# A fused attention, expert routing and feed-forward kernel: routing tables, sigmoids, transposes and the last search rearranged

## Chip, cores and metric

One core of a Trainium2 chip runs the whole program. The metric is the device time of one execution in microseconds (us), as the median of several runs.

## The reference

Three stages follow one another. Four batches of 768 positions with 8 heads of 40 make 32 (batch, head) pairs and 3072 tokens of width 320.

```python
# 1 attention, per (batch, head), step by step over t
m_new = max(f_gate + m, i_gate);  f = exp(f_gate + m - m_new);  i = exp(i_gate - m_new)
C = f*C + i*outer(v, k);  n = f*n + i*k
y = sigmoid(o_gate) * (C @ q) / max(|n . q|, 1)
# 2 routing with a capacity of 3072/8 = 384 tokens for each expert, then the expert
logits = x @ w_gate          # 8 experts
for idx in argsort(-logits.flatten()):      # best pair first
    if token not assigned and expert not full: assign
x[mask_e] = relu(x[mask_e] @ w1[e]) @ w2[e]
# 3 a gated feed-forward for all tokens
out = (sigmoid(x @ w_gate2) * (x @ w_val)) @ w_out
```

## The kernel before

**Attention** works in 6 chunks of 128 positions. A chunk has three head groups of 12, 12 and 8 (batch, head) pairs, so there are 18 steps `j`, with `c, s = divmod(j, 3)`. Within a chunk the recurrence is written as a masked matrix. For four heads at a time, `decay` (L209) makes the exponents in a PSUM tile `pg` (two buffers) with matmuls, and ScalarE turns them into weights with four `Exp` instructions (L220) in an SBUF tile `ee` (seven buffers). `score` (L223) multiplies them by q times k, `outp` (L269) applies them to v, `inter` and `state` carry the state from chunk to chunk, and `comb` (L280) multiplies by the output gate `ON[c]`, a sigmoid of a whole 128x1280 tile (`sig`, L136), on GpSimd. `gates` (L139) makes the running maxima and sums on VectorE, once for chunk 0 and once for chunks 1 to 5 together. The mask matrix `tris` (L442) is read by every `decay`.

`xout` (L298) normalizes the output y; `half` (L325) stores it to DRAM and calls `flip` (L315), which transposes blocks of 128 columns into the PSUM tile `tr` (one buffer) and copies them to the SBUF tile `xt` (one buffer). `lmm` (L331) makes the routing logits from `xt`, and `Routing.start` (L536) reduces the logits of one chunk and compares them with the first table.

`step` (L365) walks a fixed list of calls (`ORDER`, L363), in which decays run two steps ahead of the step that they belong to. In this part of the program the order of instructions on each engine is not the order of the code: a planner simulates the program and picks, of the instructions that are ready, the one traced first. Only dependencies and buffers bind it.

`Attention.run` (L343) traces the constants of the routing (`Routing.consts`, L436: 23 small VectorE instructions and 7 on GpSimd, among them the six tables `tab` of L452) ahead of everything else, then `setup` (L50: loads of the gates, of the first step's keys, queries and values, a GpSimd fill of the two key tiles `kb` at L62, the load of the first output gate, `gates(0, 1)`), `setup2` (L100: a GpSimd fill and six small loads of the router's weight `wgt`), step -1 (only decays and scores of the first steps), the sigmoid of chunk 0, steps 0 and 1, the lambdas, and steps 2 to 18. From step 2 on, `prep_moe2` (L731) is called at each `s` of the list: it splits the weights of stage 3 into pairs of numbers. The output gates of the later chunks are loaded at `LO` and put through the sigmoid at `SG`, at the end of chunks 0, 2 and 4.

**Routing and experts** run in a hand-written order (`manual_schedule`, L1120). The eight experts are taken in the order in which they fill up. `Routing.phase(i)` (L543) finds which expert is next and the logit at which it is full: six rounds, each with a comparison of all best logits with a table of thresholds on VectorE (L533), 24 small matmuls that count (L587) and one that spreads the result (L597). It then makes the list of the expert's 384 tokens (L652 to L686), and `gather` (L910) fetches them by indirect DMA. The phase for expert i+1 is a generator that `drive` (L1093) advances by one `yield` at each `yield` of `Ffn.run(i)` (L964), so that its work lies between the matmuls of expert i.

`Ffn.run(i)` does the two expert matrices (L977 to L1002) and then stage 3 in 12 blocks `f` of 128 columns: gate and value matmuls (L955 to L962), sigmoid (L1050), product (L1062), a split into two parts (L1063, L1057), and, two blocks later, nine matmuls (L1071 to L1073) that add block k = f - 2 to three token tiles `oc[tb]`. At the end each token tile is copied to SBUF (L1081, L1083) and written out by an indirect DMA from GpSimd (L1085).

Of the kernel before, what the change touches and what calls it, by code (L numbers as in the profile page):

```python
# [40 lines left out]
class Attention:  # L41

    def __init__(self, ctx, tc, g, a, xd):
        self.tc, self.nc, self.g, self.a, self.xd = tc, tc.nc, g, a, xd
        self.one = ctx.enter_context(tc.tile_pool(name="a_one", bufs=1))
        self.wk = ctx.enter_context(tc.tile_pool(name="a_work", bufs=2))
        self.ps = ctx.enter_context(tc.tile_pool(name="a_psum", bufs=1, space=bass.MemoryType.PSUM))
        self.ON, self.QT, self.W, self.X, self.XT, self.T1, self.Y, self.PO = {}, {}, {}, {}, {}, {}, {}, {}

    def setup(self):  # L50
# [10 lines left out]
        for t in self.KB:  # L61
            nc.gpsimd.memset(t, 0.0)  # L62
        self.load(0, "kqv")
        self.load_o(0)
# [3 lines left out]
        self.load(1, "kqv")  # L68
        self.KW = one.tile([L, HS, D], FT, name="kw")
# [66 lines left out]
    def sig(self, c):  # L136
        self.nc.scalar.activation(self.ON[c], self.ON[c], AF.Sigmoid)

    def gates(self, c0, c1):  # L139
# [40 lines left out]
        nc.vector.tensor_copy(self.GB[64:96, sl], G[64:96, sl])  # L180
# [28 lines left out]
    def decay(self, j, k):  # L209
        nc = self.nc  # L210
        c, s = divmod(j, NS)
        h0 = s * HS + 4 * k
        pg = self.ps.tile([L, 4, L], FT, name="pg", bufs=2)
        nc.tensor.matmul(pg, self.g["R"].tris, self.negi[:, None, :].to_broadcast([L, 4, L]), start=True, stop=False)
        for h in range(4):
            nc.tensor.matmul(pg[:, h, :], self.sel[:, h0 + h:h0 + h + 1].to_broadcast([96, L]),  # L216
                             self.GB[:, c * L:(c + 1) * L], start=False, stop=(h == 3))
        ee = self.wk.tile([L, 4, L], FT, name="ee", bufs=7)
        for h in range(4):
            nc.scalar.activation(ee[:, h, :], pg[:, h, :], AF.Exp, bias=self.GT[:, c, h0 + h:h0 + h + 1])  # L220
        self.W[j, k] = ee
# [93 lines left out]
    def flip(self, c, z, i0, n):  # L315
        nc = self.nc
        xf = self.xf(c, z)
        if i0 == 0:
            self.XT[c, z] = self.wk.tile([L, 5, 128], FT, name="xt", bufs=1)
        p = self.ps.tile([L, 4, 128], FT, name="tr", bufs=1)  # L320
        for i in range(n):
            nc.tensor.transpose(p[:, i, :], xf[:, 128 * (i0 + i):128 * (i0 + i) + 128], self.g["ident"])
        nc.scalar.activation(self.XT[c, z][:, i0:i0 + n], p[:, :n], AF.Copy)
# [7 lines left out]
    def lmm(self, c, z, i0, n):  # L331
        if i0 == 0:
            self.PL = self.ps.tile([L, 7, 2, E], FT, name="pic", bufs=2)
        for i in range(i0, i0 + n):
            self.nc.tensor.matmul(self.PL, self.XT[c, z][:, i, :], self.wgt[:, i][:, None].to_broadcast([L, 7, 2, E]),
                                  start=(i == 0), stop=(i == 4))
# [28 lines left out]
    def step(self, j, side):  # L365
# [7 lines left out]
        if j == -1:  # L373
            for k in range(n1):
                self.decay(0, k)
        for t in self.ORDER:
            if t == "L" and cur and nx2:
                self.load(j + 2, "kqv")
            elif t == "LO" and cur and s < 2 and c % 2 == 0 and c + 1 + s < NC:
# [21 lines left out]
            elif t == "KW" and nxt:  # L401
                self.kw(j + 1)
            elif t in ("S0", "S1", "S2") and nxt and int(t[1]) < n1:
                self.score(j + 1, int(t[1]))
            elif t == "H2" and hv:
                self.half2(*hv, 2 if j == last else 0)
                if j == last - 1:
                    self.store(NC - 1, 1, 0)
                    self.flip(NC - 1, 1, 0, 2)
                if hv[1]:  # L410
                    self.g["R"].start(hv[0])
            elif t == "SG" and cur and s == NS - 1 and c % 2 == 0:
                for z in range(c + 1, min(c + 3, NC)):
                    self.sig(z)
            elif t == "s":
                side(1)


class Routing:
# [15 lines left out]

    def consts(self, tmp):  # L436
# [4 lines left out]
        self.tris = one.tile([128, 128], BF, name="tris")  # L441
        nc.vector.tensor_scalar(self.tris, jp, 0.0, None, op0=OP.is_gt)  # L442
# [100 lines left out]
    def phase(self, i, on_e, on_x):  # L543
        nc, wk = self.nc, self.wk
        v, t8, A, cmp = self.v, self.t8, self.A, self.cmp
        last = i == E - 1

        def be(t):
            return t[:, :, None].to_broadcast([128, NJ, E])

        if i:
            yield from self.best(slice(0, NJ), i)
# [51 lines left out]
        ts = tx.bitcast(FT)  # L604
# [9 lines left out]

        nc.vector.tensor_scalar(gg[:, 0], v, ts, None, op0=OP.is_ge)
        nc.vector.tensor_tensor(ag, A, be(gg[:, 0]), op=OP.mult)
        with nc.allow_low_precision(reason="counts up to 24 are exact in bfloat16"):
            nc.vector.tensor_reduce(sm[:, 0], ag.rearrange("p j e -> p e j"), axis=AX.X, op=OP.add)
        nc.vector.tensor_scalar(st, v, ts, None, op0=OP.is_gt)
        nc.vector.tensor_sub(td, gg[:, 0], st)  # L620
        yield
        yield
        yield
        p = self.ps(i)
        nc.tensor.matmul(p[:, 0:E], self.ones, sm[:, 0], start=True, stop=True)
        if i:
            nc.vector.tensor_tensor(st, st, self.act, op=OP.mult)
            nc.vector.tensor_tensor(td, td, self.act, op=OP.mult)
        nc.vector.tensor_tensor(ta, t8, st, op=OP.mult)
        nc.vector.tensor_add(self.asg, self.asg, ta)  # L630
# [3 lines left out]
        nc.vector.tensor_tensor(es, p[:, 0:E], self.rem, op=OP.is_ge)  # L634
        nc.vector.tensor_tensor(es, es, self.we[:, 0], op=OP.mult)
        nc.vector.tensor_reduce(mx, es, axis=AX.X, op=OP.max)
# [11 lines left out]
        nc.vector.tensor_scalar(esb, es, mx, None, op0=OP.is_equal)  # L648
# [57 lines left out]
class Ffn:  # L706
# [257 lines left out]
    def run(self, i):  # L964
# [73 lines left out]
        for f in range(12 + LAG):  # L1038
# [27 lines left out]
            if k >= 0:  # L1066
# [117 lines left out]
```

## Time and profile before

| | |
|---|---|
| median of 3 runs | 866.32 us (865.43 to 867.01) |
| the profiled execution, its own time | 863.38 us |
| its span, first to last instruction | 861.6 us |
| TensorE (PE) busy | 803.2 us, 93% |
| VectorE (DVE) busy | 541.1 us, 63% |
| ScalarE (ACT) busy | 340.6 us, 40% |
| GpSimd (POOL) busy | 234.1 us, 27% |
| mean granted TensorE clock | 0.973 of full speed |

The span starts at 0. Attention reaches to about 200 us, the first routing search to about 223 us, and the eight experts from there to the end. A row of a timeline gives start and duration, the line in the code, the operation, output tile and inputs, sizes, and in brackets the idle time of the engine ahead of it with what ended it. Starts of consecutive matmuls lie closer than their durations, because they are pipelined: the distance of the starts is what one costs. SPq is the queue that issues the loads.

### The profile page before, as it was taken

How to read it: one execution, taken by the hardware profiler on the slowest of the kernel's cores; microseconds unless marked ns; L12 is line 12 of the kernel's file. 1: busy time of each engine (PE TensorE's matmuls, PEld its weight loads, DVE VectorE, ACT ScalarE, POOL GpSimd, SP SyncE). 2: the span in 40 equal slices, each digit the busy share in tenths (PEclk: the TensorE clock that was granted, in tenths of full speed). 3: DMA queues.
4: the chain of work that ended last, by engine and by line, in shares of the span. 5: the costliest groups of instructions: out<-in, count | busy, mean ns of one | idle time of the engine just before them, and what ended most of it. 6: DMA issues, size and time to landing. Idle time of an engine off the chain costs nothing.

```text
span 861.6 us, 16078 instructions
## 1 busy us (share of the span) xinstructions
PE 803.2 (93%) x6200; PEld 763.4 (89%) x6200; DVE 541.1 (63%) x1438; ACT 340.6 (40%) x755; POOL 234.1 (27%) x255
## 2 busy tenths in 40 slices
PE   4979888994699999999999999999999999999996
PEld 3978788893589999999999999999999999999996
DVE  7988988956576576656666566556566665642321
ACT  4776696520342342252234225222513442252321
POOL 3244444510210260071036006301710450072001
PEclk8999989996799999999999999999999999999998
DMA  5687666400400410310050014004000500130000
GB/s 151 207 266 227 197 210 198 155 29 31 135 24 1 143 40 2 112 46 24 2 158 24 1 36 123 24 2 128 30 24 2 158 24 1 60 99 24 1 1 23
DMA packets 40951, 67.66 MB, mean 79 GB/s; under 512 B 5066, under 2 KB 29386, under 8 KB 40874
## 3 DMA queue, kind: packets, MB, share of 16 engines
q1 hardware_dynamic: 38426, 58.72, 22.4%
q0 software_dynamic: 2304, 7.87, 2.8%
q8 instruction: 48, 0.79, 0.4%
q14 instruction: 29, 0.24, 0.1%
q10 hardware_dynamic: 144, 0.05, 0.0%
HBM read 58.76 MB, written 7.86 MB: 77 GB/s over the span
## 4 chain that ended last, share of the span: by engine, by line
PE 71%; DVE 2%; DMA 2%; issue 1%; ACT 1%; SPq 1%; POOL 1%; POOLq 0%; ACTq 0%; DVEq 0%
PE mm L955 8%; PE mm L956 8%; PE mm L957 8%; PE mm L977 7%; PE mm L962 5%; PE ac L1071 5%; PE mm L961 5%; PE ac L1073 5%; PE ac L1072 5%; PE rp L587 3%; PE ac L994 3%; PE ac L996 3%; PE ac L995 3%; PE ac L1000 1%; PE ac L999 1%; DMA ws<-in_moe_w_dram 1%
## 5 line engine op out<-in xcount | busy, mean ns | idle before, releaser
L955 PE MATMUL mm<-yh,mh 128*128 128x384 f32 x384 | 134.3, 350 | 0.0
L956 PE MATMUL mm<-yh,ml 128*128 128x384 f32 x384 | 129.3, 337 | 0.0
L957 PE MATMUL mm<-yl,mh 128*128 128x384 f32 x384 | 129.2, 337 | 0.0
L915 POOL DMA_INDIRECT xg<-xd,ix x24 | 23.8, 992 | 376.8 <-DVE scr L682 372.0
L1057 DVE TENSOR_TENSOR gl<-gf,gh 128x384 fp32r<-128x384 f32 x96 | 77.2, 804 | 37.3 <-ACT gh L1063 37.0
L1050 ACT ACTIVATE sg<-mm 128x384 f32<-128x384 f32 x96 | 47.1, 490 | 133.0 <-PE mm L962 133.0
L1063 ACT ACTIVATE gh<-gf 128x384 fp32r<-128x384 f32 x96 | 50.2, 523 | 114.2 <-DVE gf L1062 114.2
L1071 PE MATMUL ac<-oh,gh 128*128 128x320 f32 x288 | 92.6, 322 | 0.0
L1073 PE MATMUL ac<-oh,gl 128*128 128x320 f32 x288 | 89.3, 310 | 0.7 <-DVE gl L1057 0.7
L1072 PE MATMUL ac<-ol,gh 128*128 128x320 f32 x288 | 89.2, 310 | 0.0
L1062 DVE TENSOR_TENSOR gf<-sg,mm 128x384 f32<-128x384 f32 x96 | 52.7, 549 | 52.2 <-ACT sg L1050 51.6
L985 ACT ACTIVATE gh<-mm 128x384 fp32r<-128x384 f32 x64 | 31.3, 491 | 117.8 <-PE ac L1000 51.1
L955 PEld LDWEIGHTS mm<-yh,mh 128*128 128x128 f32 x384 | 72.6, 189 | 0.2 <-DVE xl L896 0.2
L956 PEld LDWEIGHTS mm<-yh,ml 128*128 128x128 f32 x384 | 72.7, 189 | 0.0
L957 PEld LDWEIGHTS mm<-yl,mh 128*128 128x128 f32 x384 | 72.3, 188 | 0.0
L962 PE MATMUL mm<-pad,mr 128*128 128x384 f32 x192 | 64.8, 338 | 0.0
L961 PE MATMUL mm<-y,m 128*128 128x384 f32 x192 | 64.6, 336 | 0.0
L220 ACT ACTIVATE ee<-pg,GT 128x128 f32<-128x128 f32 x192 | 53.9, 370 | 11.8 <-PE pg L216 11.4
L229 PE MATMUL s<-qT,kb 120*128 120x128 f32 x384 | 56.0, 292 | 2.7 <-DVE ee L230 2.4
L1073 PEld LDWEIGHTS ac<-oh,gl 128*128 128x128 f32 x288 | 54.2, 188 | 0.9 <-DVE gl L1057 0.9
L1071 PEld LDWEIGHTS ac<-oh,gh 128*128 128x128 f32 x288 | 54.6, 190 | 0.0
L278 PE MATMUL po<-vn,ee 128*128 128x123 f32 (+2 forms) x384 | 52.3, 284 | 2.2 <-DVE ee L230 2.2
(281 smaller groups left out, 1919.5 us busy)
## 6 DMA issues: line engine op xcount, KB each, us to landing
ws<-in_moe_w_dram SPq DMA_DIRECT2D x15, 480.0 KB
ws<-in_moe_w_dram SPq DMA_DIRECT2D x14, 512.0 KB
ws<-in_moe_w_dram SPq DMA_DIRECT2D x18, 256.0 KB
on<-in_on_dram SPq DMA_DIRECT2D x6, 640.0 KB
xd<-y SPq DMA_DIRECT2D x24, 160.0 KB
st<-in_moe_w_out_dram SPq DMA_DIRECT2D x12, 320.0 KB
st<-in_moe_w_gate_dram SPq DMA_DIRECT2D x8, 384.0 KB
st<-in_moe_w_val_dram SPq DMA_DIRECT2D x8, 384.0 KB
```

Of the source, the lines that this page charges most:

```text
L220: nc.scalar.activation(ee[:, h, :], pg[:, h, :], AF.Exp, bias=self.GT[:, c, h0 + h:h0 + h + 1])
L229: nc.tensor.matmul(s[:, h, :], self.KB[j % 2][:, a, r, :], self.QT[j][:, a, :], start=True, stop=True)
L955: mm(p, wh[:, d, cs], h[:, d], start=(d == 0), stop=False)
L956: mm(p, wl[:, d, cs], h[:, d], start=False, stop=False)
L957: mm(p, wh[:, d, cs], l[:, d], start=False, stop=False)
L961: mm(p, w2[:, cs], x[2], start=False, stop=False)
L962: mm(p, wr[:, c2], self.pad[z], start=False, stop=True)
L977: mm(p, (self.al if t == 1 else self.ah)[:, d, cs], x[t // 2][:, d], start=(d == 0 and t == 0), stop=False)
L1057: nc.vector.tensor_tensor(gl, hs[f - 1][0], hs[f - 1][1].bitcast(FT), op=OP.subtract)
L1071: mm(o, gh[:, ts], self.oh[:, k], start=(k == 0), stop=False)
L1072: mm(o, gh[:, ts], self.ol[:, k], start=False, stop=False)
L1073: mm(o, gl[:, ts], self.oh[:, k], start=False, stop=(k == 11))
```

## The change

- **Routing tables.** `Routing.consts` is traced after step 1 instead of first, its temporary tiles move to the pool that opens after the gates' pool closes, and each of its VectorE instructions is held by an ordering edge (`issue_after`) behind the last VectorE instruction of `gates(0, 1)`. `tris` is made early, by a function of its own. `setup2` moves behind step 1, too.
- **Start.** The fills of `kb` go from GpSimd to ScalarE, as copies of the identity scaled by 0. The first loads come in the order q, v, k. Step -1 is written out: `kw(0)`, decays and scores of step 0, decays of step 1, then step 0. The output gate of chunk 0 is loaded in step 0.
- **Sigmoids.** They come in pairs, in step 0 and at the end of chunks 1 and 3. An edge holds a pair behind the last `Exp` traced, and the `Exp` of the next four `decay` calls are held behind the pair. Output gates are loaded in odd chunks.
- **Last chunk's transposes** use `pg` (two buffers) instead of `tr` in PSUM, and tiles of the `ee` pool instead of `xt` in SBUF, one for each call of `flip`.
- **Last expert.** The phase for expert 7 does not search: all tokens still active go to it. It yields as often as before (`sum(...) + 3` empty yields).
- **End.** In the last expert's stage 3 the blocks k = 10 and 11 are added token tile by token tile, in place of block by block.

```diff
@@ Attention.setup, sig, decay, flip
-            nc.gpsimd.memset(t, 0.0)
-        self.load(0, "kqv")
-        self.load_o(0)
+            nc.scalar.activation(t.rearrange("p a r t -> p (a r) t"), g["ident"][:GP, None, :].to_broadcast([GP, 12, L]),
+                                 AF.Copy, scale=0.0)
+        self.load(0, "qvk")
...
+        g["R"].strict(g["jp"])
...
+    def sig2(self, c0, c1):
+        tc = self.tc
+        with tc.issue_after(self.lastexp):
+            ins = self.sig(c0)
+        for c in range(c0 + 1, c1):
+            with tc.issue_after(ins):
+                ins = self.sig(c)
+        self.behind = [ins, 4]
...
+        ins, n = self.behind
+        with self.tc.issue_after(ins) if n else nullcontext():
+            for h in range(4):
+                e = nc.scalar.activation(ee[:, h, :], pg[:, h, :], AF.Exp, bias=self.GT[:, c, h0 + h:h0 + h + 1])
+        self.lastexp = e.ins
+        self.behind[1] = max(0, n - 1)
...
+        end = c == NC - 1
+        p = self.ps.tile([L, 4, 128], FT, name="pg" if end else "tr", bufs=2 if end else 1)
...
+        if end:
+            t = self.wk.tile([L, 4, L], FT, name="ee", bufs=7)
@@ Attention.run
-            rt.consts(self.gp)
             self.setup()
-            self.setup2()
+            self.kw(0)
+            for k in range(GK[0]):
+                self.decay(0, k)
+                self.score(0, k)
+            gend = self.gend
             g1 = self.gates(1, NC)
-            self.step(-1, lambda n: None)
-            self.sig(0)
+            for k in range(GK[1]):
+                self.decay(1, k)
             self.step(0, lambda n: [next(g1, 0) for _ in range(2 * n)])
...
             self.step(1, lambda n: None)
+            self.setup2()
             self.lambdas()
         with self.tc.tile_pool(name="a_conv", bufs=1) as cv:
+            with self.tc.issue_after(gend):
+                rt.consts(cv)
@@ Attention.step
-            elif t == "LO" and cur and s < 2 and c % 2 == 0 and c + 1 + s < NC:
+            elif t == "LO" and j == 0:
+                self.load_o(0)
+                self.load_o(1)
+                self.sig2(0, 2)
+            elif t == "LO" and cur and s < 2 and c % 2 and c + 1 + s < NC:
...
-            elif t == "SG" and cur and s == NS - 1 and c % 2 == 0:
-                for z in range(c + 1, min(c + 3, NC)):
-                    self.sig(z)
+            elif t == "SG" and cur and s == NS - 1 and c % 2:
+                if c + 1 < NC:
+                    self.sig2(c + 1, c + 3)
@@ Routing.phase
+        ts = None
+        if not last:
+            ts = yield from self.search(i)
...
+        if last:
+            nc.vector.memset(td, 0.0)
+            nc.vector.tensor_tensor(ta, t8, self.act, op=OP.mult)
+            nc.vector.tensor_add(self.asg, self.asg, ta)
+            nc.vector.tensor_copy(mx, t8[:, 0:1])
+            for _ in range(sum(3 if n > 31 else 2 for n, _, _ in self.tab) + len(self.tab) + 3):
+                yield
@@ Ffn.run
-            if k >= 0:
+            if i == E - 1 and f >= 12:
+                if f == 13:
+                    for tb in range(3):
+                        ts = slice(tb * 128, tb * 128 + 128)
+                        o = oc[tb][:, :HD]
+                        for k in (10, 11):
+                            gl, gh = hs[k]
+                            mm(o, gh[:, ts], self.oh[:, k], start=False, stop=False)
+                            mm(o, gh[:, ts], self.ol[:, k], start=False, stop=False)
+                            mm(o, gl[:, ts], self.oh[:, k], start=False, stop=(k == 11))
+            elif k >= 0:
```

## Rows read from the trace of the kernel before

**Rows 1.** Busy time by stage: stretch, length, PE, PEld, DVE, ACT, POOL, clock, DMA.

```profile
16.00:45.00 29.00, 26.32 (x216) 23.92 (x216) 25.32 (x47) 23.43 (x65) 7.00 (x10) 0.88 0.67 207
45.00:90.00 45.00, 38.82 (x332) 35.96 (x331) 41.25 (x85) 30.18 (x86) 19.76 (x21) 0.96 0.77 248
...
180.00:193.00 13.00, 12.81 (x116) 12.69 (x115) 8.78 (x20) 1.21 (x4) 2.24 (x2) 1.00 0.01 1
...
400.00:500.00 100.00, 100.00 (x792) 95.61 (x792) 61.59 (x175) 32.66 (x63) 20.94 (x19) 1.00 0.13 40
```

**Rows 2.** PE's timeline in expert 6, around one round of the search.

```profile
710.99 0.76 PE L587 MATMUL rp<-A,cmp 128*128 128x8 bf16 x24
...
711.87 0.34 PE L977 MATMUL mm<-xh,al 128*128 128x384 f32 x1
712.04 0.34 PE L977 MATMUL mm<-xl,ah 128*128 128x384 f32 x1
...
713.09 0.18 PE L597 MATMUL rp<-sat,ones 128*128 128x1 bf16 x1
...
713.38 0.34 PE L977 MATMUL mm<-xh,al 128*128 128x384 f32 x1
```

**Rows 3.** All waits of PE from 700 to 860 us: total, times, longest.

```profile
PE mm L924 <- DMA xg<-xd,ix: 0.5, 1, 0.5
```

**Rows 4.** PE's timeline, first and last of its last 18 matmuls.

```profile
850.61 0.31 PE L1071 MATMUL ac<-oh,gh 128*128 128x320 f32 x1
...
853.11 0.31 PE L1073 MATMUL ac<-oh,gl 128*128 128x320 f32 x1
```

**Rows 5.** Timelines of DVE and POOL at the end of the span.

```profile
850.87 0.56 DVE L1057 TENSOR_TENSOR gl<-gf,gh 128x384 fp32r<-128x384 f32 x1 [0.59 <-ACT gh L1063]
...
853.29 0.97 POOL L1085 DMA_INDIRECT out_dram<-xg,ix  x1 [67.96 <-ACT xg L1083]
...
855.83 0.97 POOL L1085 DMA_INDIRECT out_dram<-xg,ix  x1 [0.22 <-issue]
```

**Rows 6.** PE's timeline, end of attention: last transposes and router matmuls.

```profile
193.53 0.66 PE L322 MATMUL tr<-ident,y 128*128 128x128 f32 x4 [0.73 <-DVE y L306]
194.94 0.33 PE L322 MATMUL tr<-ident,y 128*128 128x128 f32 x1 [0.75 <-ACT xt L323]
...
197.12 0.70 PE L335 MATMUL pic<-wgt,xt 128*128 128x112 f32 x4 [0.53 <-ACT xt L323]
...
198.73 0.92 PE L335 MATMUL pic<-wgt,xt 128*128 128x112 f32 x6 [0.58 <-ACT xt L323]
```

**Rows 7.** DVE's timeline at the start.

```profile
1.45 3.43 DVE L442 TENSOR_SCALAR tris<-jp 128x128 bf16<-128x128 f32 x1
...
5.32 0.18 DVE L499 TENSOR_SCALAR k<-tab 128x63 int32<-128x63 int32 x1
...
6.49 0.48 DVE L144 TENSOR_TENSOR_SCAN m<-gt,m 96x128 f32<-96x128 f32 x1
...
10.69 0.90 DVE L180 CAST GB<-G 32x128 bf16<-32x128 f32 x1
16.13 1.55 DVE L144 TENSOR_TENSOR_SCAN m<-gt,m 96x640 f32<-96x640 f32 x1 [4.54 <-DMA gt<-in_f_gate_dram]
```

**Rows 8.** Timelines of ACT and POOL at the start.

```profile
10.42 1.28 ACT L137 ACT_TABLE_LOAD   x1
...
16.96 5.62 ACT L220 ACTIVATE ee<-pg,GT 128x128 f32<-128x128 f32 x20
...
2.12 2.68 POOL L62 MEMSET kb<- 120x1536 f32 x2
```

**Rows 9.** Groups of ACT instructions by line, 0 to 195 us: the sigmoids and their table loads.

```profile
L137 ACT ACT_TABLE_LOAD x6 | 7.7, 1283 | 4.1 <-DMA on<-in_on_dram 4.0
L137 ACT ACTIVATE on<-on 128x1280 f32<-128x1280 f32 x6 | 7.6, 1271 | 2.7 <-DMA on<-in_on_dram 2.7
```

**Rows 10.** PE's timeline: the longest wait for an exp behind a sigmoid.

```profile
59.92 0.38 PE L214 MATMUL pg<-negi,tris 128*128 128x512 bf16 x1 [2.68 <-ACT ee L220]
```

More of the change, by code (lines that the diff above doesn't have):

```diff
@@ L1 @@
-from contextlib import ExitStack
+from contextlib import ExitStack, nullcontext
 import concourse.bass as bass
@@ L434, in alloc, with strict @@
             self.nc.gpsimd.memset(t, 0.0)
+    def strict(self, jp):
+        self.tris = self.one.tile([128, 128], BF, name="tris")
+        self.nc.vector.tensor_scalar(self.tris, jp, 0.0, None, op0=OP.is_gt)
     def consts(self, tmp):
@@ L541, in start, with search @@
         self.compare(sl, tab, n)
[L543 to L552, printed above, removed]
+    def search(self, i):
+        nc, wk, A, cmp = self.nc, self.wk, self.A, self.cmp
         P = wk.tile([128, 1], I32, name="P")
@@ L603, in phase, with be @@
         nc.vector.tensor_tensor(tx, tx, dg, op=OP.bitwise_xor)
-        ts = tx.bitcast(FT)
+        return tx.bitcast(FT)
+    def phase(self, i, on_e, on_x):
+        nc, wk = self.nc, self.wk
+        v, t8, A, cmp = self.v, self.t8, self.A, self.cmp
+        last = i == E - 1
+        def be(t):
+            return t[:, :, None].to_broadcast([128, NJ, E])
+        if i:
+            yield from self.best(slice(0, NJ), i)
+        ts = None
+        if not last:
+            ts = yield from self.search(i)
         gg = wk.tile([128, 3, NJ], BF, name="gg")
@@ L633, in phase @@
         esb = wk.tile([128, E], BF, name="esb")
-        nc.vector.tensor_tensor(es, p[:, 0:E], self.rem, op=OP.is_ge)
-        nc.vector.tensor_tensor(es, es, self.we[:, 0], op=OP.mult)
-        nc.vector.tensor_reduce(mx, es, axis=AX.X, op=OP.max)
+        if last:
[5 more added lines that the diff above has]
+                yield
+        else:
+            nc.vector.tensor_scalar(gg[:, 0], v, ts, None, op0=OP.is_ge)
+            nc.vector.tensor_tensor(ag, A, be(gg[:, 0]), op=OP.mult)
+            with nc.allow_low_precision(reason="counts up to 24 are exact in bfloat16"):
+                nc.vector.tensor_reduce(sm[:, 0], ag.rearrange("p j e -> p e j"), axis=AX.X, op=OP.add)
+            nc.vector.tensor_scalar(st, v, ts, None, op0=OP.is_gt)
+            nc.vector.tensor_sub(td, gg[:, 0], st)
+            yield
+            yield
+            yield
+            p = self.ps(i)
+            nc.tensor.matmul(p[:, 0:E], self.ones, sm[:, 0], start=True, stop=True)
+            if i:
+                nc.vector.tensor_tensor(st, st, self.act, op=OP.mult)
+                nc.vector.tensor_tensor(td, td, self.act, op=OP.mult)
+            nc.vector.tensor_tensor(ta, t8, st, op=OP.mult)
+            nc.vector.tensor_add(self.asg, self.asg, ta)
+            nc.vector.tensor_tensor(es, p[:, 0:E], self.rem, op=OP.is_ge)
+            nc.vector.tensor_tensor(es, es, self.we[:, 0], op=OP.mult)
+            nc.vector.tensor_reduce(mx, es, axis=AX.X, op=OP.max)
         mm = self.mmp[:, 1:2 * NJ + 1]
@@ L647, in phase @@
         on_e()
-        nc.vector.tensor_scalar(esb, es, mx, None, op0=OP.is_equal)
+        if not last:
+            nc.vector.tensor_scalar(esb, es, mx, None, op0=OP.is_equal)
         yield
```

41 lines of the change are left out of this document (11 added, 30 removed).

## The prediction

> **What bounds the kernel now.** I read the busy time by stage first, then the waits and timelines of the places that the change touches.
>
> The stages have different limits [rows 1]. In the expert stage (400 to 500 us) PE is busy for all of 100.00 us at full clock; DVE has 61.59, ACT 32.66. What leaves PE's queue there comes off the time; what leaves another engine does not. The steady part of attention (45 to 90 us) has two engines near their limit, DVE with 41.25 and PE with 38.82 of 45 us, and no DMA limit. The start (16 to 45 us) is like it, at a mean clock of 0.88. In the last 13 us of attention PE is the bound again, 12.81 of 13.
>
> **The last search.** The change takes six rounds of the search out of expert 6's run, where PE is full; its only wait from 700 to 860 us is 0.5 us for a gather [rows 3]. In a round the 24 small matmuls start at 710.99 and the second wide matmul behind them at 711.87: 0.88 us, of which one wide slot (712.04 - 711.87 = 0.17) is the work of expert 6, so 0.71 us are the search's [rows 2]. The one matmul that spreads the result takes 713.38 - 713.09 - 0.17 = 0.12 us. Six rounds and the count at L625 are 6 x 0.71 + 7 x 0.12 = **5.1 us**. Nothing hides PE's work here, so all of it counts. The yields stay, so the index list, the weight loads and the gather keep their distance to the matmuls of expert 6; the 0.5 us wait stays as well. Bounds: 4.3 (only the 24) to 5.6 (that wait goes, too).
>
> **The end.** The last 18 matmuls start (853.11 - 850.61) / 17 = 0.147 us apart [rows 4]. Token tile 0 is complete with the twelfth now and with the sixth after, 0.88 us earlier; but the sixth reads `gl`, which DVE ends at 850.87 + 0.56 = 851.43 [rows 5], where its slot is at 851.35, so some 0.15 is given back. POOL issues the three scatters one behind the other, 853.29 to 855.83, and the first waits for that tile's copy alone [rows 5]. All three move by **0.7 us**. If tile 2 became the late one, it would be less: bounds 0.3 to 0.9.
>
> **The last chunk's transposes.** From 193.53 to the end of the last router matmul at 198.73 + 0.92 = 199.65 PE waits three times for the copy out of the one bank or tile: 0.75, 0.53, 0.58 us [rows 6]. With two banks the second flip no longer waits, so 0.75 goes. Of the two waits in front of router matmuls, each needs its copy in any case; the transposes of the second half can be issued earlier, under the first half's router matmuls, if the planner orders them so. I take 0.75 and 0.45 of the rest: **1.2 us**. Bounds: 0.4 and 1.86, all three. This stretch hands over directly to the first search, on which everything waits, so it counts in full.
>
> **The start.** The fill of `kb` on POOL runs from 2.12 to 4.80, and the compare for `tris` on DVE, issued at 1.45, ends with it at 4.88 [rows 7, 8]. The tables queue behind it, and the first scan of the gates starts at 6.49. Without fill and tables the scan waits only for its loads; it can't gain more than that block, 3.43 us, and nothing if the loads land just then. More telling is what follows: DVE idles 4.54 us before the second scan (16.13), whose loads are issued behind that of the output gate, and ACT does its first exp at 16.96, because it loaded the sigmoid's table at 10.42 and waited for that gate [rows 7, 8], although the gates' last result was there at 10.69 + 0.90 = 11.59. After the change the exps of two steps come first and the gate loads no longer stand in front. So DVE's 4.54 us should go: -4.5. Against that, 22 table instructions return later, now in a stretch where DVE is the busiest engine: at 0.18 us for a 63-column one [rows 7] at most 4.0 us. Only those with temporary tiles must wait for the gates' pool; the others can fill the pauses behind the first gates. I put 1.2 us of them on the path. Net **3.3 us**. Bounds: -6.3 (first exp right after 11.59 less a second for its matmuls, 16.96 - 10.7) to +4.0 (tables in full, nothing gained).
>
> **The sigmoids.** Six sigmoids of 1.27 us each have a table load of 1.28 us [rows 9], and the exps behind need theirs back. Three pairs save three loads ahead and as many behind, up to 7.7 us of ACT. ACT isn't the bound, so only what PE waits for counts: at 59.92 PE stood 2.68 us before a decay's matmul because both `pg` banks waited for exps queued behind a sigmoid [rows 10]. Five of the six come after the start, two pairs will; each pair holds the exps about one sigmoid longer than a single one does. I take one such wait less, with some of the slow clock behind it (0.96 on the mean from 45 to 90 us [rows 1]), less what longer holds cost: **2.0 us**. Bounds: +3 (two pairs each hold 1.27 longer) to -4.5.
> The table load at 10.42 is 1.28 us long, and nothing else shows beside it [rows 8]. The Trainium skill, "ScalarE: Activation LUTs", section "What ACT_TABLE_LOAD costs", gives about 2.66 us for each switch with a drain, by which six saved switches would be 16.0 us of ACT rather than 7.7, and this term, scaled alike, 4.1 us.
>
> **Edits costed at nothing.** The fills of `kb` on ACT lie ahead of its first exp; they cost between 0 and the 2.68 us of POOL [rows 8], if the first keys' load, which waits for them, becomes the latest load of step 0; I take 0, since queries and values now go ahead of it. The six `wgt` loads and the output gates' loads pass behind other loads on SP's queue; if one comes late, PE or ACT stands in order behind it, for at most such a wait as the 4.54 us [rows 7]; two steps of lead cover them.
>
> **Sum.** 5.1 + 0.7 + 1.2 + 3.3 + 2.0 = 12.3 us. The profiled execution took 863.38 us (span 861.6 and 1.8 around it), so it would take 851.1; it lies 2.9 us below the median of 866.3, from which the same 12.3 leave **854.0 us**.
>
> **Rivals.**
> *Attention gives it all back.* The two terms of the start and the sigmoids vanish, because the stretch behind is paced by DVE, which gets the tables in addition: 41.25 of 45 us are full [rows 1]. Against it: the 4.54 us of idle DVE are real. Then 866.3 - 7.0 = 859.3 us. This takes in that the planner leaves the tables and transposes in about their old order, so that the change hardly does what it says in attention.
> *Attention gains in full.* All of the bounds: 5.1 + 0.7 + 1.9 + 6.3 + 4.5 = 18.5, so 847.8 us. For it: PE's waits lower the clock (0.88 at the start, where 1.00 holds later [rows 1]), so a wait that goes is worth more than its length. The price of a switch in the Trainium skill ("ScalarE: Activation LUTs", the section above) speaks for this case as well; the rows show only the load.
> *Slower: the pairs starve PE.* ACT takes its queue in order. Behind a pair stand the exps of four decays, behind these PE's next `pg` matmuls, which hold up scores and outputs in PE's queue; a pair also waits for its loads. A single sigmoid cost 2.68 us of PE [rows 10]; a pair holds 1.27 more [rows 9], and if its load is late, as the sigmoids' loads were by 4.1 + 2.7 us in all [rows 9], about 3.4 more (half of that): 7.4 us each, 22 us for three, of which at most 4.5 were paid before. With the start's gain lost, too: 866.3 - 7.0 + 17.5 = 876.8 us. It is slower from the point where the pairs cost over 7.0 us more than the single ones. Against it: weights run two steps ahead, in seven buffers, and the gates are loaded at least one step before the pair.
>
> **How the numbers follow.** Forecast 0.56, giving-back 0.20, full gain 0.16, starving 0.05, others near no change 0.03. The range takes in the first three: 847.5 to 861.5 us. About 0.2% (1.7 us) is what a measurement of this kernel can tell from no change. The first three are all faster by more: 0.92, less 0.02 for a giving-back with a loss of its own, makes 0.90; the same 0.04; slower 0.06.
>
> **What would show it.** Expert 6's run has no L587 matmuls and is 5 us shorter than the others' runs, with PE still without a gap. The last scatter starts 4.5 us behind the first of the last 18 matmuls instead of 5.2 [rows 4, 5]. From the last normalization to the last router matmul it is about 5 us instead of 6.1. The first exp comes near 11 us, DVE has no idle time of 4 us before the second scan, ACT has six or seven table loads in attention, and the long PE waits before L214 are gone or fewer than before. Wrong would be: attention that ends at 199 us or later in spite of an earlier first exp (given back), or waits of several us for exps right behind each pair (starved).

## The result, and the profile after

The changed kernel takes 852.87 us (median of 4 runs, 850.98 to 854.79), the kernel before, run beside it, 865.88 us (863.35 to 867.01): a ratio of 0.9854 [0.982, 0.9887], 13.0 us less. The forecast was 854.0 us. Its profiled execution took 853.9 us (span 852.1), 9.5 us less than the one of before. Runs of one kernel scatter: the kernel before had medians of 864.93, 862.92 and 863.97 us in the three series below, with single runs from 859.2 to 868.9. Before's profiled run lies 2.5 us under its median, the changed kernel's 1.0 us above. So the two traces differ by 3.5 us less than the medians do.

The expert stage first: PE's timeline at the start of expert 6 and of expert 7 and around the last 18 matmuls, with DVE's and POOL's at the end, in the kernel after.

```profile
699.24 0.34 PE L1025 MATMUL mm<-xh,ah 128*128 128x384 f32 x1
...
772.79 0.34 PE L1025 MATMUL mm<-xh,ah 128*128 128x384 f32 x1
...
841.77 0.31 PE L1121 MATMUL ac<-oh,gh 128*128 128x320 f32 x1
...
842.64 0.41 PE L1123 MATMUL ac<-oh,gl 128*128 128x320 f32 x1
...
842.03 0.56 DVE L1105 TENSOR_TENSOR gl<-gf,gh 128x384 fp32r<-128x384 f32 x1 [0.59 <-ACT gh L1111]
...
846.36 0.97 POOL L1143 DMA_INDIRECT out_dram<-xg,ix  x1 [0.22 <-issue]
```

The first matmul of expert 6 and of expert 7 in PE's timeline before:

```profile
702.64 0.34 PE L977 MATMUL mm<-xh,ah 128*128 128x384 f32 x1
...
781.62 0.34 PE L977 MATMUL mm<-xh,ah 128*128 128x384 f32 x1
```

Expert 6 runs for 772.79 - 699.24 = 73.55 us. Before it was 781.62 - 702.64 = 78.98 us. The gain is **5.43 us**, forecast 5.1. The 0.5 us wait for a gather [rows 3] is gone too; PE has no wait at all from 700 to 845 us. The last scatter starts 846.36 - 841.77 = 4.59 us behind the first of the last 18 matmuls, before 5.22 [rows 4, 5]: **0.63 us**, forecast 0.7. The sixth matmul waits for `gl` (842.03 + 0.56), as forecast.

The end of attention, PE's timeline of the kernel after:

```profile
192.05 0.77 PE L337 MATMUL pg<-ident,y 128*128 128x128 f32 x5 [0.73 <-DVE y L322]
193.40 1.15 PE L358 MATMUL pic<-wgt,ee 128*128 128x112 f32 x8 [0.58 <-ACT ee L346]
...
195.23 1.57 PE L358 MATMUL pic<-wgt,ee 128*128 128x112 f32 x10
```

From the first transpose to the last router matmul it is 195.23 + 1.57 - 192.05 = 4.75 us, where it was 199.65 - 193.53 = 6.12 [rows 6]: **1.37 us**, forecast 1.2. Of the three waits for a copy one is left.

This gain does not all arrive at the experts. From the last router matmul to expert 0's first matmul it is 29.31 us before and 30.41 after, 1.10 us more, because PE transposes expert 0's gathered tokens at a lower clock. Busy times by stage from the first of these transposes to expert 0's first matmul, before and after:

```profile
226.58:228.96 2.38, 2.02 (x13) 1.13 (x13) 0.02 (x1) 1.18 (x3) 0.94 (x2) 1.00 0.26 71
...
223.62:227.21 3.59, 3.29 (x13) 2.14 (x13) 0.50 (x2) 1.18 (x3) 1.52 (x3) 0.58 0.18 47
```

Expert 0's own run then is 80.07 us instead of 81.72, 1.65 less; 1.16 of it is a wait of PE for a result of POOL that the changed kernel's trace lacks. No experiment isolates either: in the fourteen traces here the first stretch lies between 29.3 and 30.9 us, with and without the new transposes, and expert 0's run between 80.1 and 82.5 us.

The rest of attention is less simple. The busy times by stage of the kernel after (stretch, length, PE, PEld, DVE, ACT, POOL, clock, DMA):

```profile
16.00:45.00 29.00, 24.44 (x195) 23.21 (x196) 21.25 (x53) 16.55 (x49) 7.02 (x11) 0.88 0.67 197
45.00:90.00 45.00, 38.92 (x319) 35.73 (x318) 39.03 (x78) 28.67 (x83) 19.55 (x21) 0.92 0.76 238
...
30.00:45.00 15.00, 15.00 (x114) 14.40 (x113) 8.20 (x23) 6.99 (x28) 3.21 (x5) 0.82 0.56 155
```

The start did not get better between 16 and 45 us: the clock is 0.88 as before, and PE, DVE and ACT have done less [rows 1]; from 45 to 90 us the clock is 0.92, where it was 0.96. The timelines of ACT, PE, DVE and SP's queue of the kernel after show why (PEld is TensorE's weight load):

```profile
3.46 2.86 ACT L63 ACTIVATE kb<-ident 120x1536 f32<-120x1536 f32 x2
...
12.13 5.26 ACT L234 ACTIVATE ee<-pg,GT 128x128 f32<-128x128 f32 x20 [4.60 <-PE pg L228]
...
19.77 1.14 ACT L234 ACTIVATE ee<-pg,GT 128x128 f32<-128x128 f32 x4 [0.40 <-PE pg L228]
20.93 1.28 ACT L139 ACT_TABLE_LOAD   x1
23.54 1.27 ACT L139 ACTIVATE on<-on 128x1280 f32<-128x1280 f32 x1 [1.32 <-DMA on<-in_on_dram]
25.70 1.27 ACT L139 ACTIVATE on<-on 128x1280 f32<-128x1280 f32 x1 [0.90 <-DMA on<-in_on_dram]
26.99 1.28 ACT L234 ACT_TABLE_LOAD   x1
28.29 1.14 ACT L234 ACTIVATE ee<-pg,GT 128x128 f32<-128x128 f32 x4
...
8.47 3.21 PEld L245 LDWEIGHTS s<-qT,kb 120*128 120x128 f32 x14 [0.16 <-DMA kb<-in_kt_dram]
...
7.84 4.03 PE L245 MATMUL s<-qT,kb 120*128 120x128 f32 x16 [0.84 <-ACT GT L184]
11.70 0.61 PE L228 MATMUL pg<-GB,sel 96*128 96x128 bf16 x8
...
29.48 0.59 PE L226 MATMUL pg<-negi,tris 128*128 128x512 bf16 x1 [4.16 <-ACT ee L234]
29.86 1.91 PE L245 MATMUL s<-qT,kb 120*128 120x128 f32 x8
31.57 3.61 PE L294 MATMUL po<-vn,ee 128*128 128x123 f32 x16
...
7.81 0.90 DVE L192 CAST GB<-G 32x128 bf16<-32x128 f32 x1
...
11.58 1.55 DVE L156 TENSOR_TENSOR_SCAN m<-gt,m 96x640 f32<-96x640 f32 x1 [1.88 <-DMA gt<-in_f_gate_dram]
...
23.46 0.67 DVE L307 COPY t<-po 128x492 f32<-128x492 f32 x1
...
37.46 0.67 DVE L307 COPY t<-po 128x492 f32<-128x492 f32 x1
...
4.97 2.62 SPq L126 DMA_DIRECT2D kb<-in_kt_dram  x3
...
17.25 0.83 SPq L135 DMA_DIRECT2D on<-in_on_dram  x2
```

DVE's timeline before, where the outputs of steps 0 and 1 are taken up:

```profile
29.37 0.67 DVE L291 COPY t<-po 128x492 f32<-128x492 f32 x1
...
37.65 0.66 DVE L291 COPY t<-po 128x492 f32<-128x492 f32 x1
```

The first exp starts at 12.13 instead of 16.96, the second scan at 11.58 instead of 16.13 [rows 7, 8], and the output of step 0 is taken up at 23.46 instead of 29.37: 5.9 us gained. Then the first pair comes. From 20.93 to 28.29 ACT does no exp, 7.4 us, of which 1.32 + 0.90 are waits for the output gates' loads. PE stands for 4.16 us, and its next matmuls start further apart: 16 of L294 take 3.61 us, 0.23 each. The granted clock from 30 to 45 us is 0.82 on the mean. Step 1's output comes at 37.46, before at 37.65. The first pair has eaten the whole gain of the start.

When the outputs of some steps are taken up (us), by DVE's timeline; "again" is the changed kernel once more, the last two are experiments below:

| step | before | after | again | pair before `comb` | fills on POOL |
|---|---|---|---|---|---|
| 0 | 29.4 | 23.5 | 23.7 | 23.5 | 22.9 |
| 1 | 37.6 | 37.5 | 36.7 | 32.1 | 31.1 |
| 4 | 69.4 | 71.5 | 70.4 | 66.1 | 64.2 |
| 8 | 112.5 | 114.2 | 112.6 | 108.4 | 104.7 |
| 17 | 193.4 | 191.9 | 189.6 | 185.4 | 183.0 |

Up to step 17, attention's own gain is 1.5 us in one trace and 3.8 in the other. The 9.5 us between the first two traces are made up of it and of the stretches above: 1.48 (attention) + 1.37 (transposes) - 1.10 + 1.65 (up to expert 0, and in it) + 5.43 (search) + 0.63 (end) = 9.46 us.

### The profile page after: what moved, and what is told of

Its sections match the earlier page's. It is cut to its first block, busy times and chain, and to the rows that moved or that the text cites. A ratio compares the mean times of both kernels' runs of the same rounds, so it can differ in the third digit from the quotient of the medians.

```text
span 852.1 us, 15713 instructions
## 1 busy us (share of the span) xinstructions
PE 800.9 (94%) x6049; PEld 761.2 (89%) x6049; DVE 519.4 (61%) x1381; ACT 334.9 (39%) x751; POOL 230.2 (27%) x253
## 4 chain that ended last, share of the span: by engine, by line
PE 72%; DVE 2%; DMA 1%; ACT 0%; issue 0%; POOL 0%; POOLq 0%; ACTq 0%; DVEq 0%
PE mm L1003 8%; PE mm L1025 8%; PE mm L1004 8%; PE mm L1005 8%; PE mm L1010 5%; PE mm L1009 5%; PE ac L1129 5%; PE ac L1131 5%; PE ac L1130 5%; PE ac L1042 3%; PE ac L1044 3%; PE ac L1043 3%; PE rp L611 3%; PE ac L1048 1%; DMA xg<-xd,ix 1%; PE ac L1047 1%
## 5 line engine op out<-in xcount | busy, mean ns | idle before, releaser
L1129 PE MATMUL ac<-oh,gh 128*128 128x320 f32 x282 | 90.6, 321 | 0.0
L1131 PE MATMUL ac<-oh,gl 128*128 128x320 f32 x282 | 87.4, 310 | 0.7 <-DVE gl L1105 0.7
L1130 PE MATMUL ac<-ol,gh 128*128 128x320 f32 x282 | 87.4, 310 | 0.0
L245 PEld LDWEIGHTS s<-qT,kb 120*128 120x128 f32 x384 | 50.6, 203 | 8.5 <-DVE GT L183 4.3
L294 PE MATMUL po<-vn,ee 128*128 128x123 f32 (+2 forms) x384 | 52.6, 287 | 4.3 <-DVE ee L246 4.2
L1034 DVE SCALAR_TENSOR_TENSOR gl<-mm,gh 128x384 fp32r<-128x384 f32 x64 | 34.6, 551 | 33.9 <-ACT gh L1033 33.4
```

The lines of the kernel that those rows point to most:

```text
L245: nc.tensor.matmul(s[:, h, :], self.KB[j % 2][:, a, r, :], self.QT[j][:, a, :], start=True, stop=True)
L1129: mm(o, gh[:, ts], self.oh[:, k], start=(k == 0), stop=False)
L1130: mm(o, gh[:, ts], self.ol[:, k], start=False, stop=False)
L1131: mm(o, gl[:, ts], self.oh[:, k], start=False, stop=(k == 11))
```

## The experiments

Medians stand beside those of the kernel before in the same series (864.93, then 862.92, then 863.97 us).

### Each part alone in the kernel before

Search alone:

```diff
-        ts = tx.bitcast(FT)
+        return tx.bitcast(FT)
...
+        ts = None
+        if not last:
+            ts = yield from self.search(i)
```

> The kernel before with the last expert's search taken out alone. The trace of the changed kernel has expert 6's run 5.43 us shorter (78.98 to 73.55). Theory: all of it is PE's time and comes off the end: 5.1 to 5.5 us less than before, ratio about 0.994. Rival: what leaves PE is waited for again at the gather of expert 7's tokens, so less than 2 us come off.

858.49 us, 0.9924 [0.9895, 0.9952], 6.6 us less. In its trace expert 6 runs for 73.86 us, 5.1 less than before, and nothing else differs by as much. The forecast 5.1 lies inside the interval (4.2 to 9.1 us). The 0.5 us wait for a gather is still there in this trace.

Transposes and the order of the last blocks alone:

```diff
-        p = self.ps.tile([L, 4, 128], FT, name="tr", bufs=1)
+        end = c == NC - 1
+        p = self.ps.tile([L, 4, 128], FT, name="pg" if end else "tr", bufs=2 if end else 1)
...
+            if i == E - 1 and f >= 12:
```

> The kernel before with the last chunk's own banks and the last expert's token tiles one behind the other. Theory: last normalization to last copy of the logits 6.0 us instead of 7.4, last scatter 0.6 us earlier: 2.0 us less in all, ratio 0.9977. Rival: the gain of the transposes is given back before expert 0 starts, because PE is then at half clock for longer (in the changed kernel 2.86 us at the end of attention were 1.75 us at expert 0's first matmul): 0.9 us less.

860.28 us, 0.9929 [0.9901, 0.9957], 6.1 us less. Its trace shows both gains as in the changed kernel, the transposes 1.37 and the scatters 0.63 us, and 2.0 us is what they explain. The interval (3.7 to 8.6) excludes it, and the trace shows no more: steps 0 and 1 come 2 us earlier than in before's (27.3 and 35.6), though nothing there was changed in the code, but step 17 comes 0.6 us later (194.0). The rival's giving back is in the trace, too: from the last router matmul to expert 0's first it is 30.30 us, before 29.31. Where the surplus of the median comes from was not settled.

The start alone (tables, fills, order of the first loads and steps; the sigmoids single):

```diff
-            rt.consts(self.gp)
             self.setup()
-            self.setup2()
...
-            self.step(-1, lambda n: None)
-            self.sig(0)
...
+            elif t == "LO" and j == 0:
+                self.load_o(0)
+                self.sig(0)
+                self.load_o(1)
```

> The kernel before with the new start alone (tables late, fills on ScalarE, order of the first steps), sigmoids single as before, that of chunk 0 in step 0 without edges. Theory: the changed kernel's start gains 4.5 us and the first pair of sigmoids (ACT away from exps from 20.9 to 28.3 us) takes 3 of them back; without the pair attention ends 3 to 5 us earlier than before. Rival: attention is paced by VectorE and takes any gain of the start back: it ends 0 to 1.5 us earlier.

863.05 us, 0.9978 [0.9961, 0.9996], 1.9 us less (0.3 to 3.4). Step 0 comes at 23.7 us, 5.7 earlier than before; step 1 at 37.0, 0.6 earlier. At step 1 the gain is lost at the same place, in another way: from 21.16 to 34.07 us three single sigmoids alternate with four exps each, with six table loads among them, and PE waits 0.85 and 2.98 us for exps. At step 17 this trace is 4.2 us ahead of before's all the same (189.15), as the theory had it; but its execution, 859.69 us, was the fastest of twelve, 3.4 us under their median, so the trace shows more than the kernel gains.

The pairs alone:

```diff
+            elif t == "LO" and j == 0:
+                self.load_o(1)
...
+            elif t == "SG" and j == NS - 1:
+                self.sig(1)
+            elif t == "SG" and cur and s == NS - 1 and c % 2:
+                if c + 1 < NC:
+                    self.sig2(c + 1, c + 3)
```

> The kernel before with the sigmoids of chunks 2 to 5 in two pairs behind exps, nothing else. Theory: one wait of 2.7 us before a decay's matmul less and a stretch at half clock less: attention ends 2 us earlier. Rival: a pair holds the exps longer than a single one and costs what the single ones did: 0 to 1 us later.

The output gates' loads move along, and the edges are in; sigmoid 1 stays single. 860.46 us, 0.9931 [0.9905, 0.9958], 6.0 us less, more than the 2.0 forecast. In its trace step 17 comes 4.4 us earlier (189.0), but PE's last transposes and router matmuls, in one bank as before, now take 196.00 + 1.62 - 189.14 = 8.5 us instead of 6.1, at a granted clock of 0.62 instead of 1.00.

The four ratios add up to 2.4% where the whole change has 1.5%. By the traces the search, the transposes and the end are worth the same alone and together; what does not add up lies in the two parts of attention and in the scatter of runs, and was not divided further.

### The changed kernel, varied

Once more, without an edit:

> The changed kernel once more, as the measure for the three beside it. Both theories: 852 to 854 us, 13 us less than before, ratio 0.985.

850.88 us, 0.9862 [0.9829, 0.9894], somewhat under the expected 852 to 854. The same code reaches the end of attention 2.4 us earlier than in the first trace; the difference arises before 95 us (step 6 at 93.2 instead of 95.6). The clock from 30 to 45 us was 0.89 instead of 0.82.

The first pair in step 1. In this kernel step 0 multiplies by the output gate without its sigmoid:

```diff
             elif t == "LO" and j == 0:
                 self.load_o(0)
                 self.load_o(1)
+            elif t == "LO" and j == 1:
                 self.sig2(0, 2)
```

> The changed kernel with the first pair of sigmoids one step later (its loads stay in step 0). Theory that the first pair eats the start's gain by waiting for its loads with exps behind it: PE's wait of 4.2 us at 29.5 goes or falls under 2 us, attention ends 2 to 4 us earlier than in the changed kernel, about 850 us. Rival, that VectorE paces attention whatever the pair does: no difference, 852 to 854 us.

850.36 us, 0.9851 [0.9816, 0.9887]: no difference from the changed kernel in the same series. In the trace step 1 comes at 32.7 us, 4.0 us earlier than in "again", and PE's waits for exps from 16 to 100 us fall from 4.9 to 0.8 us, but at step 17 only 1.5 us of it are left. The time is what the rival had expected.

The edges that hold the pairs and the exps left out:

```diff
-        with tc.issue_after(self.lastexp):
-            ins = self.sig(c0)
+        ins = self.sig(c0)
...
-        self.behind = [ins, 4]
```

> The changed kernel without the ordering edges of sigmoids and exps; the pairs are only traced one behind the other. Theory: the edges keep a pair together, without them the planner puts exps between the two and table loads go up from 7 to 9 or more, 1 to 3 us slower than the changed kernel. Rival: the edges are what makes exps wait in the first pair, without them it is 2 us faster.

855.26 us, 0.991 [0.9875, 0.9944], 4.4 us over the changed kernel of the same series (the intervals overlap). Groups of ACT by line from 0 to 200 us, in this kernel:

```profile
L139 ACT ACT_TABLE_LOAD x6 | 7.7, 1283 | 3.3 <-DMA on<-in_on_dram 3.2
...
L231 ACT ACT_TABLE_LOAD x5 | 6.4, 1283 | 0.0
```

and in the changed kernel:

```profile
L139 ACT ACT_TABLE_LOAD x3 | 3.8, 1283 | 0.1
L234 ACT ACT_TABLE_LOAD x3 | 3.8, 1283 | 0.1
L63 ACT ACT_TABLE_LOAD x1 | 1.3, 1283 | 2.2 <-issue 2.2
```

Without the edges the planner puts exps between the two sigmoids, all six loads for sigmoids come back, and PE waits 8.1 us in four places for exps (16 to 100 us). It is the edges that make the pairs.

The tables traced first again:

```diff
+            rt.consts(self.gp)
             self.setup()
...
-            with self.tc.issue_after(gend):
-                rt.consts(cv)
```

> The changed kernel with the routing tables traced first again (the fills stay on ScalarE). Theory: the tables take some 2.5 us of VectorE ahead of the first scan, which waits for its loads to 3.65 us anyway, so the first exp moves by 1 us at most and the end by 0 to 1 us. Rival: the tables were what held the start, the end moves by 2.5 us or more.

852.02 us, 0.9866 [0.9832, 0.9899]: 1.1 us over the changed kernel, which these runs can't tell from nothing. With the fill on ACT, the tables in front cost almost nothing: the first scan starts at 3.76 us instead of 3.65, the second at 11.73 instead of 11.58.

### The first pair's place, and the fills

The pair just before `comb(0)`, behind the exps that the same step traces:

```diff
-                self.sig2(0, 2)
...
             elif t == "C" and cur:
+                if j == 0:
+                    self.sig2(0, 2)
                 self.comb(j)
```

> The changed kernel with the first pair traced right ahead of the first use of its gate, behind the decays of step 0, so that the exps of two more decays go ahead of it while its loads land. Theory (the pair holds exps while ScalarE waits for its loads): PE's wait of 4.2 to 4.5 us falls to 3 or less, step 1 ends 2 to 4 us earlier and 1 us or more of it is left at the end: about 850 us, ratio 0.984. Rival (VectorE paces attention): step 1 earlier, the end as in the changed kernel within 0.5 us.

848.08 us, 0.9813 [0.9781, 0.9844]. ACT's timeline of this kernel, then its busy times by stage:

```profile
25.43 1.28 ACT L139 ACT_TABLE_LOAD   x1
26.73 2.43 ACT L139 ACTIVATE on<-on 128x1280 f32<-128x1280 f32 x2
29.17 1.28 ACT L184 ACT_TABLE_LOAD   x1
```

```profile
16.00:45.00 29.00, 27.23 (x241) 25.11 (x240) 25.67 (x63) 20.61 (x62) 8.54 (x13) 1.00 0.86 254
...
60.00:75.00 15.00, 11.14 (x96) 9.71 (x95) 15.00 (x33) 8.43 (x28) 6.60 (x7) 1.00 0.66 208
```

The pair takes 5.0 us (25.43 to 30.45) instead of 7.4, for both gates are there. The table load starts 4.5 us later, and PE no longer waits long for an exp: 0.4 us from 16 to 100 us. The clock from 16 to 45 us is 1.00. Step 1 comes 5.4 us earlier than after the change, more than the theory had. From 60 to 75 us DVE is the bound: it is busy for all of 15.00 us, after the change for 14.93. By the ratios the kernel is 3.5 to 4.2 us faster than the changed one; the intervals overlap, and the changed kernel was not run in this series.

The first pair split, sigmoid 0 before `comb(0)`, sigmoid 1 at the end of chunk 0:

```diff
-                self.sig2(0, 2)
...
+                if j == 0:
+                    self.sig2(0, 1)
                 self.comb(j)
...
+            elif t == "SG" and j == NS - 1:
+                self.sig2(1, 2)
```

> The changed kernel with the first pair taken apart: the sigmoid of chunk 0 ahead of its first use, that of chunk 1 at the end of chunk 0, both behind exps. Theory: the first hold is shorter by one sigmoid and one wait for a load (2.2 us), a second one of 3.8 us is added later, where weights run ahead: as the pair ahead of its first use, or 1 us better. Rival: every visit of its own costs PE its two table loads: 1 to 2 us worse than that.

852.38 us, 0.9875 [0.9841, 0.9908]. Step 1 is earlier still (31.0 us), with nine table loads instead of seven; at step 17 (187.8) it is 2.4 us behind the unsplit pair. Splitting does not pay: it is 4.3 us over the unsplit pair in the same series, where theory and rival had expected 2 us at most.

The later sigmoids single again, the first pair left:

```diff
-            elif t == "LO" and cur and s < 2 and c % 2 and c + 1 + s < NC:
-                self.load_o(c + 1 + s)
+            elif t == "LO" and cur and s == 0 and 0 < c < NC - 1:
+                self.load_o(c + 1)
...
-            elif t == "SG" and cur and s == NS - 1 and c % 2:
-                if c + 1 < NC:
-                    self.sig2(c + 1, c + 3)
+            elif t == "SG" and cur and s == NS - 1 and 0 < c < NC - 1:
+                self.sig(c + 1)
```

> The changed kernel with the sigmoids of chunks 2 to 5 single, one at the end of each chunk, without edges, the first pair kept. Theory (each visit costs PE a wait): 4 visits in place of 2, 9 or 10 table loads in place of 7 (the first at the start), 2 us slower than the changed kernel, ratio 0.988. Rival: a pair costs what two singles cost: no difference.

855.33 us, 0.9896 [0.9867, 0.9925], with eleven table loads. Its interval overlaps with that of the changed kernel, and step 17 (191.8) is where it was after the change (191.9, 189.6): the worth of the later pairs, 0 by the traces and up to 3.6 us by the ratios, was not settled.

The fills of `kb` on GpSimd, as before:

```diff
-            nc.scalar.activation(t.rearrange("p a r t -> p (a r) t"), g["ident"][:GP, None, :].to_broadcast([GP, 12, L]),
-                                 AF.Copy, scale=0.0)
+            nc.gpsimd.memset(t, 0.0)
```

> The changed kernel with the fills of the key tiles on GpSimd again. Theory: a compare on VectorE is held until the fills end near 4.8 us, as before, so the first scan starts near 5 us instead of 3.65 and the first exp 1 us later; the end moves by less than 1 us, since the first pair follows. Rival: the fills on ScalarE delay the key loads, with GpSimd the first scores come earlier and the end with them by 1 us.

846.67 us, 0.9811 [0.9776, 0.9846], the fastest kernel of all. The timelines of POOL, DVE, PE and ACT at its start, with SP's queue:

```profile
1.06 2.69 POOL L63 MEMSET kb<- 120x1536 f32 x2
...
1.28 2.62 DVE L467 TENSOR_SCALAR tris<-jp 128x128 bf16<-128x128 f32 x1
...
4.97 0.48 DVE L155 TENSOR_TENSOR_SCAN m<-gt,m 96x128 f32<-96x128 f32 x1
...
3.14 2.62 SPq L125 DMA_DIRECT2D kb<-in_kt_dram  x3
...
6.48 1.62 PE L244 MATMUL s<-qT,kb 120*128 120x128 f32 x6 [1.32 <-DMA kb<-in_kt_dram]
...
10.29 0.79 PE L227 MATMUL pg<-GB,sel 96*128 96x128 bf16 x8
...
24.32 1.16 PE L244 MATMUL s<-qT,kb 120*128 120x128 f32 x8
25.31 1.05 PE L293 MATMUL po<-vn,ee 128*128 128x123 f32 x8
27.55 0.38 PE L225 MATMUL pg<-negi,tris 128*128 128x512 bf16 x1 [1.19 <-ACT ee L233]
...
10.89 4.23 ACT L233 ACTIVATE ee<-pg,GT 128x128 f32<-128x128 f32 x16 [1.41 <-PE pg L227]
```

and the stretch of the start in its busy times by stage:

```profile
16.00:45.00 29.00, 27.15 (x245) 25.18 (x244) 25.82 (x62) 18.63 (x54) 7.35 (x12) 1.00 0.84 266
```

The fill on POOL ends at 3.75 us, that on ACT at 3.46 + 2.86 = 6.32. Each is two fills, and the first keys' loads wait for the first of them alone; they are issued from 3.14 us on instead of 4.97. After the change PE's row of the scores names `GT` as what it waited for, which was done at 7.30 + 0.22 = 7.52 us; the row of its weight loads names the keys. In PE's queue 16 score matmuls (4.0 us) stand ahead of the matmuls from `GB`. After the change they start at 7.84 and hold these until 11.70, although `GB` was there at 8.71; here they start at 6.48, and the `pg` matmuls at 10.29. So the first exp comes 1.24 us earlier, although DVE's first scan comes 1.3 us later (4.97 against 3.65). Behind it the first pair costs PE 1.19 us instead of 4.16, and the clock stays at full. The planner's order has changed with the edit, too: 8 scores and 8 output matmuls (24.32 and 25.31) now stand ahead of the `pg` matmul that waits for the pair, where after the change scores and outputs stand behind it (29.86, 31.57). How much is the earlier load and how much this order was not separated. Step 1 comes 5.5 to 6.3 us earlier than in the changed kernel, step 17 6.6 to 8.9. By the ratios it is 3.7 to 4.4 us faster; the intervals overlap, and the changed kernel was not run in this series. The theory missed: it is the rival's mechanism, at about four times the rival's size.

## Why the prediction was right, and where it was not

**The search, the end and the transposes** were right by mechanism and size in their own stretches: 5.43, 0.63 and 1.37 us in the trace against 5.1, 0.7 and 1.2. Where PE is the only bound, counted matmuls times the distance of their starts gave the time within 0.4 us. The surplus of the search goes with the 0.5 us gather wait that was expected to stay: in the search alone, where it stays, the gain is 5.12. Of the transposes the step "so it counts in full" is not borne out: 1.10 us came back before expert 0 in this trace, at the lower clock.

**Attention's sum** (3.3 + 2.0 = 5.3 us) is about right by the medians, not shown by the traces. From the 13.0 us of the medians 5.4 + 0.6 + 1.4 = 7.4 are taken; 5.6 us remain, in which the 1.10 us given back and the 1.65 of expert 0 are contained, too. The two traces of the changed kernel show 1.5 and 3.8 in attention, against a trace of before that is 2.5 us short. So that the whole came out 0.7 us from the forecast is in part luck: an attention that gained less than 5.3 in both traces, 1.65 us in expert 0 that nobody forecast, and medians that lie further apart than the traces.

**The start's term** (3.3) failed in its division: at step 1 0.2 us of it are left in the first trace and 1.0 in the second. Its first half held: the first exp, the second scan and step 0 are earlier by 4.8, 4.6 and 5.9 us. But fill and tables, the causes named first, have no share in the time that these runs can show: taken back each by itself, the tables change it by 1.1 us, and the fill on POOL makes it shorter. The order of loads and first steps, which is left, was not run alone. (The bound of -6.3 takes the matmuls' time off 11.59, where it comes on top.) What I overlooked is that the slower rival's mechanism would strike here once. I costed the moved sigmoids as one wait less and gave the starving pairs 0.05, as if all three pairs starved PE or none did. The first pair kept ACT from exps for 7.4 us; PE stood 4.16 us and lost more to the clock behind, and step 1 lost the 5.4 us that the same pair at another place gives back, near that rival's 7.4 for a pair. Late loads are in it: the output gates' loads are issued at 17.25 us by SP's queue, and ACT was ready for them at 20.93 + 1.28 = 22.21. That "the gates are loaded at least one step before the pair", the reason against the rival, was false for this pair. With the pair before `comb(0)` the gates are there in time; that experiment and the one with the pair in step 1 show the cause of the loss at step 1. So "two steps of lead cover them", said of these loads under the edits costed at nothing, failed as well. How much of it lasts differs: 1.5 of 4.0 us (against the second trace) at step 17 in step 1's variant, and with the pair before `comb(0)` about all of it, 4.2 to 6.5 us. DVE is full from 60 to 75 us in both, the bound that the giving-back rival named; why one variant keeps its gain and the other does not is not shown.

**The fills costed at nothing** were the wrong choice of value. The prediction named the condition, "if the first keys' load, which waits for them, becomes the latest load of step 0", and took 0. It is late enough: PE's weight loads wait for it, and the matmuls that the exps need stand behind. The cost, by taking the edit back, is 3.7 to 4.4 us by ratios and more by the traces, above the bound of 2.68. The bound took the fill's length; it left out that the edit also moves the planner's order around the first pair, and with it PE's wait there (4.16 against 1.19) and the slow clock. In which proportion is open.

**The sigmoids' term** (2.0) can't be told from 3 to 6: alone 6.0 [3.6 to 8.2], as the edges' worth in the changed kernel 4.4, as the later pairs' 0 to 3.6. The price of a switch can be read, though: the exps that start at 19.77 end at 20.91, and the load follows at 20.93 for 1.28 us. The Trainium skill, "ScalarE: Activation LUTs", "What ACT_TABLE_LOAD costs", gives 2.66 us with a drain; the trace shows no drain between, and the measurement decides for 1.28.

**The signs.** Seven table loads, DVE's pause before the second scan 1.88 us instead of 4.54, expert 6 without the search and no gap of PE: as forecast. The first exp at 12.13 instead of "near 11": the fill. PE's waits before the decays from 16 to 100 us: 6.3 us in three before, 4.2 in one after, fewer but longer. One of the three, 3.45 us at 18.15 us behind the first sigmoid, is longer than the 2.68 that [rows 10] gives as the longest; the starving rival priced a single sigmoid too low by that. Its sign, a wait of several us right behind a pair, was there behind the first pair only.

## What to carry to other kernels

What a full engine has to do less of can be counted from the distance of its starts and comes off the time; a gain at the start of a pipelined stage holds only as far as the next held queue, so follow it step by step to the end of the stage. Before moving a fill to a free engine, look at the load that waits for it and at what stands behind that load's first reader in its queue. A batch of work on an in-order engine goes behind the work that others wait for, and after its own loads are there.

## What the runs showed of the hardware

- A GpSimd fill (1.06 to 3.75 us) holds two small VectorE compares that read one operand: 2.69 and 2.62 us, 0.26 and 0.22 with the fill on ACT. The Trainium skill, "SBUF — State Buffer", "SBUF: two separate sides", says that the two engines share a port pair, which a GpSimd instruction, or a VectorE instruction in a mode that uses two ports, holds for its whole length while the other is blocked; the rows agree, but the mode of these compares is in no trace. Unexpected was that being rid of this cost time.
- After PE's stop of 4.16 us its matmuls of 128x123 started 0.23 us apart, where eight of them took 1.05 us in the kernel with the fills on POOL, 0.13 each. The granted clock was 0.82 from 30 to 45 us, and 1.00 in the four variants of the changed kernel in which PE waited 1.2 us at most for an exp from 16 to 100 us (pair in step 1, before `comb(0)`, split, fills on POOL).
- PE's stretch with the transposes of expert 0's gathered tokens, the same matmuls each time, took 2.38 us at a granted clock of 1.00 and 3.59 at 0.58.
- The same program, run twice, differed by 2.4 us at the end of attention, all of it from the first 95 us.

**The better versions.** The changed kernel with the fills back on GpSimd (846.67 us) and the one with the first pair before `comb(0)` (848.08 us) have lower medians than both kernels, before and after. They change different lines; the two together were not tried.
